# V loads of a low-rank attention kernel moved to a second DMA queue

## The chip, the cores and the metric

The kernel runs on one core of one Trainium2 chip. The metric is the device time of one execution in microseconds (us). The trace and the profile of an execution come from the hardware profiler. An execution is called fast or slow by its time; on one core "slow" only means over 1.5% above the fastest execution of the same kernel.

Engines are written as the profile writes them: PE is TensorE (matmuls), DVE is VectorE, ACT is ScalarE, SP is SyncE. SPq and ACTq are the instruction streams that issue DMA loads. Each has its own queue (q1 and q10 on the page after), and both put their loads on the same 16 DMA engines.

## The reference

One query per head, 32 heads, a K and a V of 8192 x 256 per head (bf16). K and V are first projected along the sequence to 8 rows, then there is an ordinary softmax over those 8 rows.

```python
B, H, Sq, Skv, Dh, R = 2, 16, 1, 8192, 256, 8
kp = jnp.einsum("rn,bhnd->bhrd", e_proj, k)
vp = jnp.einsum("rn,bhnd->bhrd", f_proj, v)
scores = jnp.einsum("bhqd,bhrd->bhqr", q, kp) * (Dh ** -0.5)
p = softmax(scores, axis=-1)
o = jnp.einsum("bhqr,bhrd->bhqd", p, vp)
```

K and V are 268.4 MB together and each byte is used once, so the time is that of reading them.

## The kernel before

The work goes in 16 pairs of tiles. A pair is K and V of two heads: 8.39 MB of K in the buffer `kt`, 8.39 MB of V in the buffer `vt` (128 partitions x 64 KiB each). There is one buffer for K and one for V. Matmuls use a tile once, and then the buffer is free to be loaded again.

SyncE issues all loads, in the order K0, V0, K1, V1, ..., on its one queue:

```python
for a in range(NP):                                   # NP = 16 pairs
    if a > 0:
        nc.sync.wait_ge(s_kr, a)                      # K of pair a-1 has been used
        nc.sync.dma_start(out=kt[:], in_=k_t[a]).then_inc(s_kd, 16)
    else:
        ...                                           # K0 in two halves, the small inputs between
    if a > 0:
        nc.sync.wait_ge(s_vr, a)                      # V of pair a-1 has been used
    if a < NP - 1:
        nc.sync.dma_start(out=vt[:], in_=v_t[a]).then_inc(s_vd, 16)
    else:
        ...                                           # the last V in six pieces
```

TensorE runs K, softmax, V of one pair after the other, in program order:

```python
with nc.tensor.Fori(0, NP) as it:
    ...                                               # q of this pair
    nc.tensor.wait_ge(s_kd, tk)                       # K has landed
    for i in range(J // 2):                           # 64 matmuls, L225 (L221 in the kernel after)
        mm = nc.tensor.matmul(tile4(acc_k, i % CT), lhsT=rows(wk, i), rhs=rows(kt, i), ...)
    mm.then_inc(s_kr, 1)                              # kt is free
    ...                                               # scores; DVE and ACT make the softmax
    nc.tensor.wait_ge(s_w, t1)                        # the weights from the softmax
    nc.tensor.wait_ge(s_vd, tv)                       # V has landed
    for i in range(SPREAD // 2):                      # 56 matmuls, L236 (L232 after)
        ...
        mm = nc.tensor.matmul(o_4[...], lhsT=rows(wq, i), rhs=rows(vt, i), ...)
    mm.then_inc(s_o4, 1)                              # ACT copies o_4 out, PE folds it (L246)
    ...
    for j in range(SPREAD, J):                        # 32 matmuls, L252 (L248 after)
        ...
    mm.then_inc(s_vr, 1)                              # vt is free
```

ScalarE's loop per pair: copy q, exponential, copy `o_4`.

## Time and profile before

| | before |
|---|---|
| time | 629.22 us, median of 3 runs (629.08 to 629.37) |
| bytes read | 268.7 MB, 428 GB/s over the span |
| DMA engines' packets | 99.2% of sixteen engines' span |
| PE busy | 35% |

These lines are from the page of the kernel before: the mean busy share of the DMA engines (tenths) and what they moved in 40 slices of the span; the one queue with its packets, MB and share of sixteen engines' time; the chain of waits by engine.

```profile
DMA  9999999999999999999999999999999999999997
GB/s 375 445 434 434 426 443 401 468 401 468 401 468 401 468 401 468 401 468 401 468 401 468 401 459 409 451 417 451 417 451 417 426 443 417 451 409 459 401 434 302
...
q1 hardware_dynamic: 5856, 268.73, 99.2%
...
DMA 80%; PE 17%; ACT 2%; issue 1%; SPq 0%; DVE 0%
```

The DMA engines are full from end to end, with one queue, and the chain is mostly a wait for DMA. One stretch of the span between the first K matmul of one pair and that of the next, by the view of busy times in a stretch (stretch and its length; busy us of the engines; the granted TensorE clock; the DMA share; GB/s):

```profile
core 0: us, PE busy (x) PEld busy (x) DVE busy (x) ACT busy (x) POOL busy (x), PEclk, DMA share, GB/s
217.65:256.35 38.70, 13.60 (x164) 5.66 (x164) 4.95 (x13) 1.53 (x4) 0.00 (x0) 0.68 1.00 434
```

A pair takes 38.70 us, with the DMA share at 1.00 and 434 GB/s. In the packet records of the trace a packet of K or V is 64 KiB and takes 2.42 us; an engine has eight per tile, one right after the other.

The timeline of the kernel before around a V and the next K (start us, us, engine, line, operation, output<-input, count, idle time before and what ended it):

```profile
237.01 5.74 PE L236 MATMUL o<-vt,wq 128*4 128x512 bf16 x56 [12.19 <-DMA vt<-in_v_dram]
...
243.97 1.09 PE L252 MATMUL o_x<-vt,wp 128*32 128x128 bf16 x32
...
245.09 0.33 SPq L177 DMA_DIRECT2D vt<-in_v_dram  x1
...
256.35 5.06 PE L225 MATMUL acc_k<-kt,wk 128*32 128x512 bf16 x64 [10.98 <-DMA kt<-in_k_dram]
...
261.46 0.33 SPq L166 DMA_DIRECT2D kt<-in_k_dram  x1
```

V is used from 237.01 us and its buffer is loaded again by an issue at 245.09, 8.1 us later (7.53 us in the mean of 15 pairs). K is used from 256.35 and reissued at 261.46, 5.1 us later (the 64 matmuls take 5.6 us in the mean of 16). Neither delay costs anything: when V is reissued at 245.09, the next K is still in flight and lands only at 256.35, and the other way round. So the issue-to-landing times of the page are more than a third waiting behind the other tile (operation, count, median us from issue to landing):

```profile
vt<-in_v_dram SPq DMA_DIRECT2D x15, 31.2
kt<-in_k_dram SPq DMA_DIRECT2D x15, 33.0
```

They are 31 to 33 us for a tile that needs 19.35 us of DMA time. PE waits about equally for V and for K (us in total, times, longest):

```profile
PE o L236 <- DMA vt<-in_v_dram: 180.6, 17, 12.8
PE acc_k L225 <- DMA kt<-in_k_dram: 173.1, 15, 12.2
```

### The profile page before, as it was taken

The numbers are of one execution on the slowest core, as the hardware profiler recorded it, in microseconds if no ns is written. First come the engines' busy times: TensorE is split into PE (matmuls) and PEld (weight loads), VectorE is DVE, ScalarE is ACT, GpSimd is POOL, SyncE is SP. The second block draws the span as 40 slices with busy tenths as digits, with TensorE's granted clock in tenths as the row PEclk, the third lists the DMA queues.
The fourth block names the chain that finished last, engine by engine and source line by source line (L and its number), as shares of the span: only waits on it lengthen the run. The fifth ranks groups of instructions, "written<-read, shape, count | busy, mean of one in ns | idle before, by whom it ended". The sixth has DMA issues, their size and how long they took to land.

```text
span 627.9 us, 6257 instructions
## 1 busy us (share of the span) xinstructions
PE 218.0 (35%) x2690; PEld 94.7 (15%) x2690; DVE 83.9 (13%) x221; ACT 27.9 (4%) x68; POOL 14.8 (2%) x20
## 2 busy tenths in 40 slices
PE   0732443222443224332243421444313343223434
PEld 0411111011211112111011210111101121011211
DVE  2020201102011020200202002020020200202002
ACT  0200000000000000000000000000000000000000
POOL 9000000000000000000000000000000000000000
PEclk9767676577765677756677566766567765577667
DMA  9999999999999999999999999999999999999997
GB/s 375 445 434 434 426 443 401 468 401 468 401 468 401 468 401 468 401 468 401 468 401 468 401 459 409 451 417 451 417 451 417 426 443 417 451 409 459 401 434 302
DMA packets 5857, 268.73 MB, mean 428 GB/s; under 512 B 673, under 2 KB 1121, under 8 KB 1377
## 3 DMA queue, kind: packets, MB, share of 16 engines
q1 hardware_dynamic: 5856, 268.73, 99.2%
q14 instruction: 1, 0.00, 0.0%
HBM read 268.71 MB, written 0.02 MB: 428 GB/s over the span
## 4 chain that ended last, share of the span: by engine, by line
DMA 80%; PE 17%; ACT 2%; issue 1%; SPq 0%; DVE 0%
DMA vt<-in_v_dram 80%; PE o L236 13%; PE o_x L252 2%; PE o_x L246 2%; ACT o_sb L274 2%; SPq L181 0%; SPq L172 0%; SPq L171 0%; SPq L170 0%; SPq L173 0%; SPq L169 0%; DVE o_sb L320 0%; SPq L346 0%; SPq L110 0%
## 5 line engine op out<-in xcount | busy, mean ns | idle before, releaser
L225 PE MATMUL acc_k<-kt,wk 128*32 128x512 bf16 x1024 | 90.0, 529 | 173.1 <-DMA kt<-in_k_dram 173.1
L236 PE MATMUL o<-vt,wq 128*4 128x512 bf16 x896 | 84.0, 552 | 184.7 <-DMA vt<-in_v_dram 180.6
L225 PEld LDWEIGHTS acc_k<-kt,wk 128*32 128x32 bf16 x1024 | 33.5, 128 | 225.0 <-DMA kt<-in_k_dram 176.1
L236 PEld LDWEIGHTS o<-vt,wq 128*4 128x4 bf16 x896 | 25.8, 112 | 236.2 <-DMA vt<-in_v_dram 183.8
L295 DVE SCALAR_TENSOR_TENSOR prod<-acc_k,q_sb 128x512 f32<-128x512 f32 x16 | 11.1, 692 | 260.2 <-PE acc_k L225 260.2
L291 DVE MEMSET wp<- x16 | 1.4, 85 | 232.7 <-PE o_x L252 230.3
L274 ACT COPY o_sb<-o 128x512 f32<-128x512 f32 x16 | 9.4, 585 | 260.0 <-PE o L236 260.0
L303 DVE TENSOR_TENSOR wtmp<-fw,p 128x1024 f32<-128x1024 bf16 x16 | 19.6, 1226 | 6.8 <-ACT p L272 6.8
L307 DVE TENSOR_REDUCE wp<-wtmp 128x128 f32<-128x1024 f32 x16 | 19.5, 1220 | 0.0
L252 PE MATMUL o_x<-vt,wp 128*32 128x128 bf16 x512 | 17.4, 219 | 0.0
L272 ACT ACTIVATE p<-ps_e,nmax 128x8 f32<-128x8 f32 x16 | 4.3, 267 | 281.5 <-DVE nmax L301 281.5
L252 PEld LDWEIGHTS o_x<-vt,wp 128*32 128x32 bf16 x512 | 16.3, 97 | 0.0
L246 PE MATMUL o_x<-o_sb,foldw 128*32 128x128 f32 x128 | 10.1, 275 | 12.6 <-ACT o_sb L274 12.6
L229 PE MATMUL ps_e<-scr,gmask 128*128 128x8 f32 x32 | 6.2, 266 | 18.4 <-DVE scr L298 18.4
L200 PE MATMUL ps_e<-st,sel 128*128 128x128 bf16 x32 | 7.0, 272 | 15.2 <-DMA st<-in_f_proj_dram 14.2
L270 ACT CAST q_sb<-q_ps 128x512 bf16<-128x512 f32 x16 | 9.4, 585 | 30.9 <-PE q_ps L219 30.9
L311 DVE TENSOR_SCALAR wq<-wp,rs 64x112 bf16<-64x112 f32 x32 | 9.2, 288 | 2.0
L246 PEld LDWEIGHTS o_x<-o_sb,foldw 128*32 128x32 f32 x128 | 6.3, 108 | 20.3 <-issue 20.3
L229 PEld LDWEIGHTS ps_e<-scr,gmask 128*128 128x128 f32 x32 | 4.8, 188 | 26.3 <-DVE scr L298 26.3
L315 DVE TENSOR_SCALAR wp<-wp,rs 64x16 f32 x32 | 8.3, 258 | 0.7
L200 PE MATMUL ps_f<-st,sel 128*128 128x128 bf16 x32 | 6.8, 274 | 0.0
L219 PE MATMUL q_ps<-q,sel_q 32*128 32x256 bf16 x32 | 6.5, 281 | 0.2 <-issue 0.2
(38 smaller groups left out, 51.2 us busy)
## 6 DMA issues: line engine op xcount, KB each, us to landing
kt<-in_k_dram SPq DMA_DIRECT2D x2, 4096.0 KB, 16.4
vt<-in_v_dram SPq DMA_DIRECT2D x1, 4096.0 KB, 21.0
vt<-in_v_dram SPq DMA_DIRECT2D x1, 2048.0 KB, 25.5
vt<-in_v_dram SPq DMA_DIRECT2D x1, 1024.0 KB, 27.6
vt<-in_v_dram SPq DMA_DIRECT2D x1, 640.0 KB, 28.7
vt<-in_v_dram SPq DMA_DIRECT2D x1, 256.0 KB, 28.9
vt<-in_v_dram SPq DMA_DIRECT2D x15, 31.2
kt<-in_k_dram SPq DMA_DIRECT2D x15, 33.0
```

The lines of the kernel that those rows point to most:

```text
L200: mm = nc.tensor.matmul(ps[:, bass.ds(r, 1), :].rearrange("p o j -> p (o j)"), lhsT=pick, rhs=st[:, i, x, :], start=(x == 0), stop=(x == X ...
L225: mm = nc.tensor.matmul(tile4(acc_k, i % CT), lhsT=rows(wk, i), rhs=rows(kt, i), start=(i < CT), stop=(i >= J // 2 - CT), skip_group_check ...
L229: nc.tensor.matmul(s_ps, lhsT=gmask[:].rearrange("k g p -> k (g p)"), rhs=scr[:], start=True, stop=True).then_inc(s_sp, 1)
L236: mm = nc.tensor.matmul(o_4[(i % CT) * W:(i % CT) * W + 2 * G, :], lhsT=rows(wq, i), rhs=rows(vt, i), start=(i < CT), stop=(i >= SPREAD // ...
L246: nc.tensor.matmul(tile4(o_x, x)[:, 0:DX], lhsT=foldw[:, b, :], rhs=o4_sb[:, b * Dh + x * DX:b * Dh + (x + 1) * DX], start=False, stop=Fal ...
L252: mm = nc.tensor.matmul(tile4(o_x, x)[:, 0:DX], lhsT=wp[:, j - SPREAD, :], rhs=vt[:, j, x * DX:(x + 1) * DX], start=False, stop=(j == J - ...
L270: nc.scalar.copy(out=q_sb[:], in_=q_ps[:]).then_inc(s_qa, 1)
L274: nc.scalar.copy(out=o4_sb[:], in_=o_4[:]).then_inc(s_ev, 1)
L295: nc.vector.scalar_tensor_tensor(out=prod[:], in0=acc_k[:], scalar=scale, in1=q_sb[:], op0=ALU.mult, op1=ALU.mult, accum_out=sc[:]).then_i ...
L303: nc.vector.tensor_tensor(out=wtmp[:], in0=fw[:], in1=p32[:].unsqueeze(1).to_broadcast([P, J, R]), op=ALU.mult).then_inc(s_d[1], 1)
L307: nc.vector.reduce_sum(out=wp32[:], in_=wtmp[:], axis=AX.X).then_inc(s_d[3], 1)
L311: mk = nc.vector.tensor_scalar(out=wq[lo:hi, :, g], in0=wp32[lo:hi, 0:SPREAD], scalar1=rs[lo:hi], scalar2=None, op0=ALU.mult)
```

## The change

The intent: K through SyncE's queue and V through ScalarE's, half a tile apart, so that the two loads overlap. Only the last V stays on SyncE's queue.

```diff
-            if a > 0:
-                nc.sync.wait_ge(s_vr, a)
-            if a < NP - 1:
-                nc.sync.dma_start(out=vt[:], in_=v_t[a]).then_inc(s_vd, 16)
-            else:
-                ... the last V in six pieces
+        nc.sync.wait_ge(s_vr, NP - 1)
+        ... the last V in six pieces, after the loop
@@ ScalarE
+        nc.scalar.wait_ge(s_k0, 16)                  # the first half of K0 has landed
+        nc.scalar.dma_start(out=vt[:], in_=v_t[0]).then_inc(s_vd, 16)
         ...
+        with nc.scalar.Fori(0, NP - 2) as it:
+            t1 = nc.scalar.snap(it + 1)
+            scalar_step(t1)                          # the three operations as before
+            nc.scalar.wait_ge(s_vr, t1)
+            nc.scalar.dma_start(
+                out=vt[:], in_=v_next[bass.ds(it, 1)].rearrange("a q j d -> (a q) j d")).then_inc(s_vd, 16)
+        scalar_step(NP - 1)
+        scalar_step(NP)
```

More of the change, by code (lines that the diff above doesn't have):

```diff
@@ L173 @@
                 nc.sync.dma_start(out=kt[:, j0:J], in_=k_t[a][:, j0:J]).then_inc(s_kd, 16)
-            if a > 0:
-                nc.sync.wait_ge(s_vr, a)
-            if a < NP - 1:
-                nc.sync.dma_start(out=vt[:], in_=v_t[a]).then_inc(s_vd, 16)
-            else:
-                j0 = 0
-                for js, s in zip(LAST_V, s_vl, strict=True):
-                    nc.sync.dma_start(out=vt[:, j0:j0 + js], in_=v_t[a][:, j0:j0 + js]).then_inc(s, 16)
-                    j0 += js
+        nc.sync.wait_ge(s_vr, NP - 1)
+        j0 = 0
+        for js, s in zip(LAST_V, s_vl, strict=True):
+            nc.sync.dma_start(out=vt[:, j0:j0 + js], in_=v_t[NP - 1][:, j0:j0 + js]).then_inc(s, 16)
+            j0 += js
         nc.sync.wait_ge(s_fin, X)
@@ L266, with scalar_step @@
         nc.scalar.copy(out=fw[:], in_=ps_f[:].rearrange("p r j -> p j r")).then_inc(s_f0, 1)
-        with nc.scalar.Fori(0, NP) as it:
-            t1 = nc.scalar.snap(it + 1)
+        def scalar_step(t1):
             nc.scalar.wait_ge(s_q, t1)
@@ L274 @@
             nc.scalar.copy(out=o4_sb[:], in_=o_4[:]).then_inc(s_ev, 1)
+        v_next = v_t[1:NP - 1]
+        with nc.scalar.Fori(0, NP - 2) as it:
[6 more added lines that the diff above has]
+        scalar_step(NP)
         nc.scalar.wait_ge(s_vr, NP)
```

## The prediction

> **What bounds it.** The DMA engines. The page's 40 slices show DMA at 9 tenths in all but the last; queue 1's packets take 99.2% of sixteen engines' span; the chain of waits is 80% V loads; PE is busy 35%. By the timeline, V loads are issued at 50.79 and 553.51 us, thirteen tile pairs apart: 38.67 us per 16.78 MB pair, 434 GB/s. The trace's packets are 64 KiB, 2.42 us each, eight per engine and tile (19.35 us), without gaps. [...] 268.7 MB at 434 GB/s is 619 us; the other 9 are start and tail. There is nothing to win in the middle.
>
> **What the change does.** It removes no work. Before, one first-in first-out queue: when K lands, a whole V (19.35 us) stands behind it, so consuming and reissuing K is hidden. After, two queues are served together: [...] Each tile then takes up to 38.7 us, and one queue runs alone while the other's buffer is consumed.
>
> Those gaps, from the timeline: K lands, 64 matmuls (mean 5.63 us), reissue, first packet 1.25 us after issue (as at the start): about 7.1 us with landing delay. V lands, 56 matmuls, copy 0.59, folds, 32 matmuls, reissue (mean 7.53), first packet: about 9.1 us. V's gap is 2 us longer. With equal sharing V loses that to K each turn, so the distance from K's landing to V's grows, in steps of packets, from the half tile it starts with. Once the next K lands inside V's gap, both queues are empty together, and PE takes V, then K, in program order: some 2 us of idle DMA per pair (an estimate).
>
> **Sum (estimate from those durations).** Start: V0 is issued only when K's first half has landed (13 us); K's second half, in 32 KiB packets, alternates with V's 64 KiB ones, so K0 lands near 37 us; V0 then waits for K0's softmax: 1 to 2 us of idle DMA near 42 us. Middle: some five pairs without loss while the phase drifts, then ten at 1.5 to 2 us: 15 to 20. End: the last V queues behind the last K; the 6 us tail stays. 629 + 2 + 15 = 646 us.
>
> **Predicted: 646 us, range 629 to 664. Faster by over 2%: 0.01; within 2%: 0.35; slower by over 2%: 0.64.**
>
> **What would show it.** Bandwidth in the slices below 434 GB/s in the later two thirds, with short holes just after V's landings. Issue to landing takes 30 to 39 us with nothing queued ahead. The distance from K's to V's landing grows from about 20 to 33 us and stays. PE's waits before K's matmuls vanish late in the run; those before V's grow. If the phase stays and the slices stay at 434, the time is about 631.
>
> **What would make it wrong.** Whole packets decide the drift: K's gap is 2.9 packets, V's 3.8. If rounding makes both the same number, the phase locks where no hole is: 630 to 633 us. If the engines don't share equally, or two streams together run below 434 GB/s, the loss is larger or comes from the first pair on. ScalarE's computed address could lengthen V's gap by tenths, and hasten the drift.

## The result, and the profile after

| | before | after |
|---|---|---|
| time | 629.31 us, median of 6 runs (629.08 to 629.91) | 699.42 us, median of 6 runs (692.07 to 707.76) |
| ratio of the fast runs | | 1.1028, 95% interval 1.1002 to 1.1054 |
| span of the profiled run | 627.9 us | 690.2 us (a fast run) |
| DMA packets, share of sixteen engines' span | 99.2% | 48.2% + 43.1% |

A ratio here is the mean time of one kernel's fast runs over that of the other's fast runs of the same rounds, so it is not quite the ratio of the medians. Three of the six runs after were fast (692.07 to 695.31).

The same lines of the page after:

```profile
DMA  9989999999998997979979799798897997979966
GB/s 400 406 365 425 425 448 456 433 425 425 425 425 365 448 448 289 452 308 425 425 300 429 304 425 425 304 425 365 365 425 304 425 425 304 425 304 425 425 273 274
...
q1 hardware_dynamic: 3696, 142.90, 48.2%
q10 hardware_dynamic: 2160, 125.83, 43.1%
...
DMA 80%; PE 16%; ACT 1%; issue 1%; DVE 1%; SPq 0%; ACTq 0%; DVEq 0%
```

There are now two queues, q1 (SyncE) and q10 (ScalarE). Up to about slice 12 the slices are as full as before, but for the third (the late start of V0); from there on about one in three holds some 300 GB/s and the DMA tenths fall to 7 or 8. The stretches from one pair's first K matmul to the next pair's say it in numbers (pair 2, pair 5, pair 10; the last line is the K matmuls of pair 6 alone):

```profile
core 0: us, PE busy (x) PEld busy (x) DVE busy (x) ACT busy (x) POOL busy (x), PEclk, DMA share, GB/s
109.24:145.52 36.28, 14.16 (x164) 5.79 (x164) 4.95 (x13) 1.53 (x4) 0.00 (x0) 0.64 1.00 434
220.58:264.58 44.00, 10.73 (x165) 5.01 (x164) 4.88 (x14) 1.53 (x4) 0.00 (x0) 0.61 0.90 381
441.61:485.94 44.33, 11.34 (x165) 5.15 (x165) 4.96 (x14) 1.53 (x4) 0.00 (x0) 0.62 0.89 378
264.58:268.22 3.64, 3.64 (x65) 1.61 (x64) 0.28 (x2) 0.59 (x1) 0.00 (x0) 1.00 0.87 288
```

Pair 2, with both queues running, has a DMA share of 1.00 and 434 GB/s: two streams at once lose no bandwidth. Pairs 5 and 10 take 44.0 and 44.3 us at a share of 0.90 and 0.89. From K of pair 5 to K of pair 15 the trace after takes 442.8 us (220.58 to 663.37) and the trace before 387.0 us (217.65 to 604.68). That is 55.8 of the 62.3 us between the two spans. The rest: K of pair 1 starts 8.3 us later, pairs 1 to 4 take 5.4 us less (K runs ahead there while V falls behind), and from K of pair 15 to the end it takes 3.6 us more.

What happens in such a pair, in the timeline:

```profile
257.08 4.94 PE L232 MATMUL o<-vt,wq 128*4 128x512 bf16 x56 [31.34 <-DMA vt<-in_v_dram]
...
263.24 1.09 PE L248 MATMUL o_x<-vt,wp 128*32 128x128 bf16 x32
...
264.51 0.34 ACTq L278 DMA_DIRECT2D vt<-in_v_dram  x1
...
264.58 3.64 PE L221 MATMUL acc_k<-kt,wk 128*32 128x512 bf16 x64
...
268.27 0.33 SPq L166 DMA_DIRECT2D kt<-in_k_dram  x1
```

When PE has finished V of pair 5 (264.3 us), K of pair 6 has already landed, so its matmuls start with no wait at 264.58. V is reissued at 264.51, and K only at 268.27, after the K matmuls. Between the landing of K and the first packet of the new V there is nothing to transfer: by the packet records the last K packet ends at 261.85 and the first V packet starts at 265.47; in between no DMA engine has anything. PE's waits have moved accordingly:

```profile
PE o L232 <- DMA vt<-in_v_dram: 384.2, 17, 31.3
PE acc_k L221 <- DMA kt<-in_k_dram: 49.0, 5, 13.8
```

It waits for K only in the first five pairs (49.0 us, before 173.1), and for V 384.2 us in place of 180.6. From issue to landing a tile now takes 36 to 37 us although nothing of the same queue stands ahead of it:

```profile
vt<-in_v_dram ACTq DMA_DIRECT2D x15, 36.3
kt<-in_k_dram SPq DMA_DIRECT2D x15, 37.3
```

How the kernel gets there is in the distances from the start of the K matmuls to the start of the V matmuls, read from PE's timeline, in us; pairs 0 to 14:

```
before  16.6 19.4 19.5 19.4 19.4 19.4 19.4 19.4 19.4 19.4 19.4 19.4 19.4 19.4 19.4
after   11.4 19.3 19.4 24.2 31.4 36.5 36.4 36.3 36.4 36.3 36.2 36.3 36.4 36.4 36.2
```

One queue holds the distance at 19.4 us, half of a pair. With two queues it grows until pair 5, and there it stays. Below, the growth is called the drift, the state in which it stays the lock, the pairs in that state locked pairs, and the time without a packet in such a pair the hole. This was the predicted picture; only the size of the hole was not.

### The profile page after: what moved, and what is told of

It is laid out like the page before. It is cut to its first block, busy times and chain, and to the rows that moved or that the text cites. A ratio compares the mean times of both kernels' runs of the same rounds, so it can differ in the third digit from the quotient of the medians.

```text
span 690.2 us, 6281 instructions
## 1 busy us (share of the span) xinstructions
PE 200.4 (29%) x2690; PEld 91.0 (13%) x2690; DVE 83.9 (12%) x221; ACT 28.0 (4%) x68; POOL 14.8 (2%) x20
## 3 DMA queue, kind: packets, MB, share of 16 engines
q1 hardware_dynamic: 3696, 142.90, 48.2%
q10 hardware_dynamic: 2160, 125.83, 43.1%
## 4 chain that ended last, share of the span: by engine, by line
DMA 80%; PE 16%; ACT 1%; issue 1%; DVE 1%; SPq 0%; ACTq 0%; DVEq 0%
DMA vt<-in_v_dram 75%; PE o L232 12%; DMA kt<-in_k_dram 5%; PE o_x L248 2%; PE o_x L242 2%; ACT o_sb L271 1%; PE acc_k L221 1%; DVE wtmp L310 0%; DVE wp L314 0%; ACTq L278 0%; SPq L177 0%; DVE prod L302 0%; SPq L172 0%; SPq L171 0%; SPq L170 0%
## 5 line engine op out<-in xcount | busy, mean ns | idle before, releaser
L232 PE MATMUL o<-vt,wq 128*4 128x512 bf16 x896 | 86.3, 564 | 388.4 <-DMA vt<-in_v_dram 384.2
L221 PE MATMUL acc_k<-kt,wk 128*32 128x512 bf16 x1024 | 69.9, 434 | 49.0 <-DMA kt<-in_k_dram 49.0
L221 PEld LDWEIGHTS acc_k<-kt,wk 128*32 128x32 bf16 x1024 | 28.7, 108 | 84.9 <-DMA kt<-in_k_dram 50.4
L310 DVE TENSOR_TENSOR wtmp<-fw,p 128x1024 f32<-128x1024 bf16 x16 | 19.6, 1225 | 6.8 <-ACT p L269 6.8
L314 DVE TENSOR_REDUCE wp<-wtmp 128x128 f32<-128x1024 f32 x16 | 19.5, 1220 | 0.0
## 6 DMA issues: line engine op xcount, KB each, us to landing
vt<-in_v_dram ACTq DMA_DIRECT2D x15, 36.3
```

What stands on the lines that cost most here:

```text
L232: mm = nc.tensor.matmul(o_4[(i % CT) * W:(i % CT) * W + 2 * G, :], lhsT=rows(wq, i), rhs=rows(vt, i), start=(i < CT), stop=(i >= SPREAD // ...
L310: nc.vector.tensor_tensor(out=wtmp[:], in0=fw[:], in1=p32[:].unsqueeze(1).to_broadcast([P, J, R]), op=ALU.mult).then_inc(s_d[1], 1)
L314: nc.vector.reduce_sum(out=wp32[:], in_=wtmp[:], axis=AX.X).then_inc(s_d[3], 1)
```

## The experiments

All kernels below are written out (the loops over pairs unrolled), so that every wait is for a constant. The first two, e1 and e2, are controls. The times of before beside them were 629.3 to 629.5 us. "Both empty" is the time in which no DMA engine has a packet of K or V, from the packet records of the trace. In the views a packet counts in the stretch in which it starts, so a DMA share can come out a little over 1.

### e1: the kernel before, written out

```diff
-        with nc.tensor.Fori(0, NP) as it:
-            t1 = nc.tensor.snap(it + 1)
+        for it in range(NP):
+            t1 = it + 1
             ... (the same for ScalarE and VectorE)
```

> A control: the kernel before, with its loops written out so that every wait is for a constant. Both theories expect the time of before, 629 us within 0.5%, and no gap in the DMA. If it differs by more, later runs are compared with this one instead.

Measured: 634.79 us (633.69 to 635.04), ratio 1.0079. That is 0.8%, a little more than expected. The page shows what is new in the DMA queues: 20 packets, 0.33 MB, of the kind `instruction` on a queue q8 that the page before does not have.

```profile
q1 hardware_dynamic: 5856, 268.73, 98.4%
q8 instruction: 20, 0.33, 0.2%
```

Whether they make the 5 us is not shown. The written-out experiments are compared with 634.8 us.

### e2: the changed kernel, written out

The same edit on the changed kernel; ScalarE's loads now have fixed addresses.

> A control: the changed kernel with its loops written out, so ScalarE's V loads also have fixed addresses. The theory of the closing gap (V's buffer is empty longer than K's, so the two streams drift until both are empty together) expects 690 to 710 us, the last eleven or so tile pairs at about 44 us each. The rival that ScalarE's computed address costs the time expects about 630 to 640 us.

Measured: 690.16 us, ratio 1.0918 from its three fast runs (686.65 to 690.16, at and just under the expected band; two slow runs at 698.67 and 711.89). In the profiled run, one of the slow ones, the distance grows 11.9, 17.0, 19.5, 24.3, 32.0, 36.6 and stays, and the locked pairs take 43.8 to 45.0 us. The computed address plays no part.

### e3: K reissued later, by 2 us

```diff
-                nc.sync.wait_ge(s_kr, a)      # after K's last matmul
+                nc.sync.wait_ge(s_ex, a)      # after the exponential of that K
```

> The changed kernel (written out), with one wait made LATER: SyncE reissues K after ScalarE's exponential of that K instead of after K's last matmul, about 2.05 us later by the trace of before (609.65 to 611.70). Nothing else. The theory of the closing gap: V's buffer is empty about 2 us longer than K's, so this makes the two equal, the drift stops, the two queues are never empty together after the start, and the time falls to 632 to 640 us although work was only delayed. The rival that two streams at once, or ScalarE's queue, cost bandwidth expects no gain: 690 to 715 us.

Measured: 671.44 us, ratio 1.0682, four runs (666.38 to 674.26). Delaying one load by 2 us took 17 us off e2 (means of the fast runs: 670.9 and 688.2). A loss of bandwidth from two streams alone does not explain that. But it missed the 632 to 640 us. The waits of PE show why:

```profile
PE acc_k L220 <- DMA kt<-in_k_dram: 328.7, 16, 26.0
PE o L231 <- DVE wq L313: 50.2, 13, 3.9
PE o L231 <- DMA vt<-in_v_dram: 17.4, 4, 7.3
```

In 13 of 16 pairs V now has to wait for its weights (`wq`, made by DVE from the softmax of K), not for its load. The distance from K to V sat at 10.7 to 12.0 us in pairs 0 to 11, which is the least it can be: the K matmuls plus the softmax. V had landed and could not be used. So the drift was not stopped, it was held at the other end: now K is the late one, V's buffer stands full, and V's reissue waits for K. By the packet records 0.8 to 4.7 us of DMA per pair were idle in these pairs, in the mean over the sixteen engines; moments with all of them idle were found in only two of the pairs (0 and 4).

### e4: the queues exchanged

The edit, in words:

```diff
-    K tiles from the second on: nc.sync, after s_kr;  V tiles: nc.scalar, after s_vr
+    K tiles from the second on: nc.scalar, after s_kr;  V tiles from the second on: nc.sync, after s_vr
```

> The changed kernel (written out) with the queues exchanged: K tiles from the second on go through ScalarE's queue, V tiles through SyncE's (the first V stays on ScalarE's). Buffers are empty as long as before. The theory of the closing gap expects the same loss, 685 to 715 us. The rival that ScalarE issues V late, [...] expects the loss to move or vanish: under 650 us, or K's reissue visibly late.

The rival's reason is cut: no run shows it.

Measured: 692.91 us median; one run at 672.43, three at 689.97 to 695.98. The profiled run, a slow one, has the same lock from pair 5 on: its pair 7 takes 44.20 us at a DMA share of 0.89, as with the queues the other way round. The run at 672.43 lies below the expected band; no profile of it was taken, so what it did differently is not known. But no run came near 650 us, and the profiled one locks as before. Which engine issues which stream does not decide it.

### e5: K reissued later, by 1 us

```diff
-                nc.sync.wait_ge(s_kr, a)
+                nc.sync.wait_ge(s_sc, a)      # after VectorE's scaled score of that K
```

> As the run that reissued K after the exponential (2.05 us later; 671 us, and there the distance from K's to V's landing sat at its other end, 11 us, where V waits for K's softmax), but K is reissued only about 1.1 us later, after VectorE's scaled score of that K. The theory (the side whose buffer is empty longer falls behind) says 2.05 us was too much, since V's excess is nearer 1.5 us once the durations of PE in these runs are used (7.2 against 5.7), so here neither side should fall behind for long: 632 to 665 us, faster than both 690 and 671, the idle DMA per pair under 1 us in most pairs. If any delay of K simply helps in proportion, half the delay gives about 680 us.

Measured: 659.23 us median, from 648.40 to 694.17: two runs fast (648.40, 655.83), two slow (662.63, 694.17). The fast runs lie in the expected band. The profiled run, the fast one at 655.83 us, shows both kinds of pair:

```profile
core 0: us, PE busy (x) PEld busy (x) DVE busy (x) ACT busy (x) POOL busy (x), PEclk, DMA share, GB/s
119.13:159.93 40.80, 13.08 (x165) 5.53 (x165) 4.94 (x13) 1.53 (x4) 0.00 (x0) 0.63 0.96 407
519.27:558.14 38.87, 12.29 (x165) 5.33 (x166) 4.94 (x13) 1.53 (x4) 0.00 (x0) 0.68 1.01 432
```

In pairs 1 to 10 (the first stretch is pair 2) the distance was 11.3 to 12.2 us, the end where V waits for the softmax: a share of 0.96. From pair 11 on (second stretch, pair 12) it was 14.6 to 14.8 us, away from both ends: a share of 1.01 and 38.87 us, no loss at all. So nearly equal waits can remove the loss. The four pairs lasted to the end of the run; whether anything would have held the distance there is not shown, and ten pairs of the same run stayed at the other end. That the slow run at 694 us went to the other end is likely, but no profile of it was taken.

### e6: V reissued later, first try

```diff
             nc.scalar.wait_ge(s_vr, t1)
+            for i in range(3):
+                nc.scalar.copy(out=idle[:, i], in_=o4_sb[:])
             nc.scalar.dma_start(...)
```

> The changed kernel (written out) with V reissued about 1.8 us later: ScalarE does three further copies of 0.59 us into a tile nobody reads before it issues V. The theory: V's buffer is empty 1.8 us longer, so the phase closes sooner and every locked pair loses 1.8 us more, 6.7 us in place of 4.9: 708 to 735 us. If the loss were a matter of bandwidth with two streams, 1.8 us on one stream that has slack would cost nothing: 685 to 700 us.

Measured: 691.95 us; its fast runs took 687.25 to 695.78, as e2. The experiment did not do what it was meant to. ScalarE's timeline:

```profile
301.36 0.62 ACT L274 COPY idle<-o_sb 128x512 f32<-128x512 f32 x1 [1.71 <-PE o_x L248]
301.37 0.34 ACTq L275 DMA_DIRECT2D vt<-in_v_dram  x1
301.89 1.13 ACT L274 COPY idle<-o_sb 128x512 f32<-128x512 f32 x2
```

The load was issued at 301.37 us, beside the first copy and not after the third. So in this trace the instruction that issues the load did not wait for the copies ahead of it on the same engine; no semaphore asked for that (e9 adds one). The run counts as a repetition of e2.

### e7: the start of the change alone

```diff
+            if 0 < a < NP - 1:                # later V again on SyncE's queue, behind K
+                nc.sync.wait_ge(s_vr, a)
+                nc.sync.dma_start(out=vt[:], in_=v_t[a]).then_inc(s_vd, 16)
-            nc.scalar.wait_ge(s_vr, t1)
-            nc.scalar.dma_start(out=vt[:], in_=v_t[it + 1]).then_inc(s_vd, 16)
```

> Only the start of the change: the first V through ScalarE's queue after K's first half; every later V on SyncE's queue behind K as before. This prices the late first V. From the trace of the changed kernel 2.7 to 3.5 us of idle DMA in the first pair: 637 to 640 us against 634.8 of the control written out, and no idle DMA later. The rival that the late start is the main loss expects over 670 us.

Measured: 637.43 us (636.79 to 637.96), 2.6 us over e1. The stretches of pair 0 and pair 5:

```profile
core 0: us, PE busy (x) PEld busy (x) DVE busy (x) ACT busy (x) POOL busy (x), PEclk, DMA share, GB/s
38.07:67.27 29.20, 13.23 (x164) 5.59 (x164) 4.94 (x13) 1.53 (x4) 0.00 (x0) 0.68 0.85 360
222.32:261.19 38.87, 14.31 (x164) 5.75 (x164) 4.93 (x13) 1.53 (x4) 0.00 (x0) 0.63 1.00 432
```

Pair 0 has the idle DMA (share 0.85), pair 5 has none (1.00). The distance is 19.4 to 19.6 us in pairs 1 to 14: one queue restores it at once, although the start was shifted.

### e8: V refilled in halves

Two queues. V's buffer has two halves with a semaphore each; ScalarE issues the first half of the next V as soon as the first 32 matmuls have used it. K is sent as two loads at once, to have packets of the same size (32 KiB, as K0's halves have in the trace before).

```diff
+            mm.then_inc(s_ra, 1)              # PE, after matmul 31 of V
+            nc.scalar.wait_ge(s_ra, t1)
+            nc.scalar.dma_start(out=vt[:, 0:JH], in_=v_t[t1][:, 0:JH]).then_inc(s_va, 16)
             ...                               # copy of o_4
             nc.scalar.wait_ge(s_vr, t1)
-            nc.scalar.dma_start(out=vt[:], in_=v_t[it + 1]).then_inc(s_vd, 16)
+            nc.scalar.dma_start(out=vt[:, JH:J], in_=v_t[it + 1][:, JH:J]).then_inc(s_vb, 16)
```

> Two queues kept, but V's buffer is refilled in two halves: its first half is issued on ScalarE's queue as soon as the matmuls of that half are done, while the second half is still being consumed or still in flight; K is sent as two halves too, so that both queues have packets of the same size (32 KiB). Then V's queue is not empty at the lock. The theory of the closing gap expects the loss to go: 635 to 648 us, with idle DMA only in the first pair. The rival that two queues at once are slow in themselves, or that smaller packets cost, expects 685 us or more.

Measured: 652.12 us, ratio 1.0376, four runs (649.89 to 656.79). About two thirds of the loss of e2 is gone, but the time missed the expected 635 to 648. What V waits for:

```profile
PE o L237 <- DVE wq L325: 61.8, 16, 3.9
PE o L237 <- DMA vt<-in_v_dram: 1.0, 1, 1.0
```

All sixteen V wait for the softmax: V runs ahead, and K, which still has one buffer refilled whole, is the late one.

### e9: V reissued later, with a wait

```diff
+            for i in range(3):
+                nc.scalar.copy(out=idle[:, i], in_=o4_sb[:]).then_inc(s_il, 1)
+            nc.scalar.wait_ge(s_il, 3 * t1)
             nc.scalar.dma_start(...)
```

> The run before this with three further ScalarE copies delayed nothing: its trace shows the V load issued at the start of the first copy (301.37 against 301.36 us), since the load did not wait for them. Here ScalarE waits for the three copies to finish before it issues V, about 1.8 us later. The theory: every locked pair loses some 1.7 us more than the 44.3 us measured, 45.5 to 46.5 us, and the lock comes a pair or two sooner: 703 to 735 us. If only bandwidth counted: 685 to 702 us.

Measured: 742.26 us, ratio 1.1783, four runs (740.00 to 744.55). ScalarE's timeline shows the copies and then the load:

```profile
329.10 1.66 ACT L275 COPY idle<-o_sb 128x512 f32<-128x512 f32 x3 [1.71 <-PE o_x L249]
330.78 0.34 ACTq L277 DMA_DIRECT2D vt<-in_v_dram  x1
```

Pair 5 of that run:

```profile
core 0: us, PE busy (x) PEld busy (x) DVE busy (x) ACT busy (x) POOL busy (x), PEclk, DMA share, GB/s
233.63:281.44 47.81, 10.69 (x166) 5.01 (x166) 4.94 (x14) 3.19 (x8) 0.00 (x0) 0.61 0.82 352
```

The lock came at pair 4, one earlier. The wait of 1.7 us cost some 3.6 us per locked pair (47.8 against about 44.2), more than expected. The packet records say why, in whole packets: V's queue was empty for 12.82 us, and K had only 4.83 us of packets (two) left after V's last data, where the kernel after has 7.59 us (three). K's reissue had not moved, so V's lead over it had shrunk. Both empty: 7.8 to 8.1 us per pair in pairs 4 to 13, in place of 3.6 to 4.5.

### e10: smaller packets

```diff
-                nc.sync.dma_start(out=kt[:], in_=k_t[a]).then_inc(s_kd, 16)
+                for h in range(0, J, JN):     # JN = J // 4; the same for V on ScalarE
+                    nc.sync.dma_start(out=kt[:, h:h + JN], in_=k_t[a][:, h:h + JN]).then_inc(s_kd, 16)
```

> The changed kernel (written out) with every K and V tile from the second K on sent as four loads of a quarter, so that packets are 16 KiB in place of 64; refills come no earlier. In the changed kernel's trace V's last completion writes come 2.41 us after V's last data, one packet of the other queue. If the completion takes its own turn between the queues' packets, that delay must fall to about 0.6 us here, and the wait of a new load for its first turn with it. The time: V is then empty 1.8 us less, but K, which now starts its turn sooner, has less left when V ends; the two nearly cancel, so 675 to 700 us, 3.5 to 5 us idle per locked pair. If the late completion alone made the loss, idle falls to 2.5 to 3 us per pair and the time to 655 to 675 us.

Measured: 704.10 us, ratio 1.1212, four runs (701.57 to 710.58); a little over the expected band. A locked pair:

```profile
core 0: us, PE busy (x) PEld busy (x) DVE busy (x) ACT busy (x) POOL busy (x), PEclk, DMA share, GB/s
268.64:312.92 44.28, 10.69 (x165) 4.98 (x165) 4.94 (x14) 1.53 (x4) 0.00 (x0) 0.61 0.90 379
```

From the packet records, one locked pair each (us):

```
                                     after    e10 (16 KiB packets)
V's last data to V's last completion  2.43     0.61
V's queue empty (data to data)       11.21     9.41
K's packets after V's last data       7.59     5.51
both empty                            3.62     3.90
```

The pair of the kernel after is its first locked one, pair 5; over the ten locked pairs both were empty for 3.6 to 4.5 us (mean 4.3), in e10 for 3.0 to 5.5 (mean 4.1). V's completion comes one packet of the other queue after its data (2.43 us, and 0.61 us in e10), so that delay shrinks with the packet. V's queue was empty 1.8 us less, and K had 2.1 us less left, so the hole stayed. The late completion by itself does not set the loss.

### e11: both refilled in halves

As e8, and K likewise:

```diff
+            nc.sync.wait_ge(s_rk, a)          # the first 32 K matmuls are done
+            nc.sync.dma_start(out=kt[:, 0:JH], in_=k_t[a][:, 0:JH]).then_inc(s_ka, 16)
             nc.sync.wait_ge(s_kr, a)
-            nc.sync.dma_start(out=kt[:], in_=k_t[a]).then_inc(s_kd, 16)
+            nc.sync.dma_start(out=kt[:, JH:J], in_=k_t[a][:, JH:J]).then_inc(s_kd, 16)
```

> As the run with V in halves (652 us, where V ran ahead until it had to wait for K's softmax, and K's queue was then still empty), but K is refilled in halves too: its first half is issued once the 32 matmuls of that half are done. Then neither queue is empty while its tile is consumed. The theory expects no idle DMA in nearly all pairs and 635 to 642 us, against 634.8 of the control. If two queues at once cost something apart from being empty together, it stays at 648 us or more.

Measured: 638.15 us, ratio 1.0135, four runs (637.54 to 639.97). The slices of its page:

```profile
DMA  9999999999999999999999999999999999999995
GB/s 378 431 428 429 429 428 428 438 434 433 432 431 432 428 431 429 428 431 434 433 432 428 431 432 433 428 433 428 433 432 431 430 429 430 431 428 431 436 396 216
```

From the second slice to the third last they hold 428 to 438 GB/s, as full as before, with two queues and half-size packets. Two queues cost next to nothing when they are not empty together: 3.4 us over e1. It does not beat the kernel before.

### e12: the first V issued at once

```diff
-        nc.scalar.wait_ge(s_k0, 16)
```

> The changed kernel (written out) without ScalarE's wait for K's first half, so the first V is issued at the start: another starting distance. The theory says the starting distance is not kept, and any start ends with both queues empty together: 655 to 705 us. If the half-tile start was chosen wrongly and a start decides, the time can fall to 640 us or less.

Measured: 701.50 us, ratio 1.1065 from three fast runs (694.36 to 703.32; one slow at 717.75). The distance grew 10.4, 14.9, 17.0, 19.4, 26.7, 33.4, 36.3 and locked. Another start, the same end.

## Why the prediction was wrong

The predicted time was 646 us with a range to 664; the runs took 692 to 708. "Slower" and the mechanism were right, the size was not.

- **The bound was right.** The DMA engines at 434 GB/s, 38.7 us per pair, and nothing to win there: with two queues pair 2 has the same 434 GB/s, and e11 takes 638.15 us against 634.79 of e1. That no run could go faster is not shown.
- **Equal sharing was right.** The packet records after alternate between the queues packet by packet (from 230 to 254 us in all 158 successions of packets that could be matched), and pair 2 has 434 GB/s so. It was an assumption when the prediction was written.
- **The start was right in kind.** Predicted: 1 to 2 us of idle DMA near 42 us, and K0 near 37. Measured: 2.3 us of both empty (42.44 to 44.75), K0 used from 38.10; by e7 the start costs 2.6 us. From 16.74 to 33.97 us K0's 32 KiB packets (1.21 us each) and V0's of 64 KiB (2.42 us) took turns, as predicted, 3.63 us a round.
- **The drift and the lock were right.** Predicted: a distance from about 20 to 33 us after some five pairs, then ten locked pairs. Measured: from 19 to 36 us by pair 5, and ten pairs from K of pair 5 to K of pair 15. The steps from pair 2 to pair 5 (19.4, 24.2, 31.4, 36.5) are 4.8, 7.2 and 5.1 us, 2.0, 3.0 and 2.1 packets of 2.42 us. That the difference of the two waits moves the distance is shown by e3, e5 (K later: the loss shrinks) and e9 (V later: it grows); that being empty together is the loss is shown by e11.
- **The step that failed: "some 2 us of idle DMA per pair (an estimate)".** It measured 3.6 to 4.5 us of both empty, 4.5 to 5.0 us in the mean over the engines, and 5.6 us of time per pair (44.3 less 38.7; DMA share 0.89 of 44.33 is 39.5 us of packets, so about 0.8 us are packets that took longer). Ten times 5.6 is 56; ten times "1.5 to 2" was 15 to 20.
- **What was missing in that term.** The term is V's gap (from V's last data to the first packet of the next V) less the time for which K's packets still fill it. The estimate took V's gap as 9.1 us; in the locked pairs it was 11.2 to 11.8. The packet records show why: after a tile's data come sixteen 4-byte packets in the same queue, here called its completion writes (in pair 5 the trace has the landing some 0.35 us after them). In pair 5 V's last data ends at 254.27 and the last of these starts at 256.69, 2.42 us later, when a packet of K has run on each engine; it is 2.41 to 2.42 us for each of the 14 V loaded through ScalarE's queue after the first. In the trace before, with one queue, the last one starts as the last data ends (V of pair 5: both 236.51).
- **The second thing missing: K's time on PE.** K was assumed to take 5.63 us of PE, the mean of the kernel before. In every locked pair, where it starts right behind V, it took 3.64 us, at a granted clock of 1.00 (the last of the stretches shown above). In the trace before, the same 64 matmuls took 5.06 us at a mean granted clock of 0.71 (from 256.35), 5.60 at 0.64 (from 217.65) and 6.14 at 0.58 (from 295.06); why the clock is 1.00 at the lock was not tested. So K is back sooner and V's lead over it, which is what K has left to fill the hole, is smaller.
- **How the two combine.** In the kernel after that second error is hidden: a new load had its first packet 2.8 to 5.7 us after its issue when the other queue was busy (the K that follows K of pair 5: issued at 224.26 us, first packet at 229.27, 5.0 us later), against 0.96 us for a V into an idle DMA (264.51 to 265.47). The difference is 1.9 to 4.8 us, up to two packets of the other queue, and that rounds the lead up to three packets. e10 makes both visible: with small packets the completion comes early, but the lead shrinks as well, and the hole stays. An estimate without packets points the same way: V's use less K's use was 7.53 less 5.63, 1.9 us, in the prediction, and is 7.4 to 8.0 less 3.64, about 3.8 to 4.3 us, in the locked pairs. No run changed K's time on PE alone, so how the miss divides between the two errors is argued, not shown.
- **A figure misread, without effect.** The prediction took 1.25 us from an issue to its first packet. The trace before has 1.00 us at the start (issue at 0.94, first packet at 1.94). It enters both gaps alike and drops out of their difference.
- **"If rounding makes both gaps the same number, the phase locks where no hole is"** did not come about in the changed kernel. e5 had such pairs (distance 14.6 to 14.8, share 1.01), its last four before the end.
- **ScalarE's computed address** made no difference to the time (e2). V's issue did come later: in the trace after 0.18 us after V's last matmul (264.33 to 264.51), in the written-out e6 with a fixed address 0.04 us (301.33 to 301.37). Whether the loop or the address makes the 0.14 us is not shown.

What stays open: why the changed kernel's runs spread over 16 us. A lock that sets in a pair or two earlier or later would do it (5.6 us each): the profile of e6 (685.5 us) locks at pair 7, that of the kernel after (690.2) at pair 5, that of e2 (696.9) already loses 2.9 us in pair 4 (mean over the engines). Single locked pairs also run longer: pair 9 of e12 took 48.04 us. No run was made to test it.

## What to carry to other kernels

A single first-in first-out queue did more here than carry the loads: it kept two streams half a cycle apart (19.4 us of 38.7, in the trace before), so that one was always in flight while the other's buffer was being used. Put on two queues that share the engines, the same two streams had no fixed distance here; the one whose buffer was empty longer fell behind until both were empty at once, or until one waited for the other's result. If two queues are wanted, give each stream a piece of buffer that can be refilled while the rest is used (e11: 638.15 us against 690.16 of e2). With the DMA already full (99.2%) the second queue gained nothing here: e11 does not beat e1's 634.79 us.
